# Scaling two query blocks from a two-byte copy, heads innermost, in a one-core kernel of linear attention and a state-space convolution

## The chip, the cores and the metric

The kernel runs on one core of a Trainium2 chip. A core has five engines that run side by side, each with its own instruction list in program order: TensorE (PE, matmuls; its weight loads are shown apart as PEld), VectorE (DVE), ScalarE (ACT), GpSimd (POOL) and SyncE (SP, which here only issues DMAs). They meet through semaphores. SBUF is the on-chip memory, PSUM the small memory that matmuls write and DVE and ACT read. The metric is the device time of one execution in microseconds (us), the median over several.

## What is computed

Two independent parts share the core, and their outputs stand side by side in the last axis (448 and 448 columns, 2048 rows):

```python
# part A: linear attention with a softmax feature map, H = 16 heads of Dh = 28
q, k, v = split(x @ wqkv)                     # x: 2048 x 448
pq, pk  = q @ w_phi[h], k @ w_phi[h]
phi_q = concat(softmax(pq), softmax(-pq))     # 56 features a head
phi_k = concat(softmax(pk), softmax(-pk))
kv  = phi_k^T v ;  z = sum over rows of phi_k
num = phi_q kv  ;  den = phi_q z + 1e-6
a   = (num / den) @ wo
# part B: S4 state-space convolution, 448 channels, 256 complex states
K = Re sum_n C_n B_n dt exp(dt A_n l)         # l = 0 .. 2047
b = causal convolution of u with K  +  u * Dskip
return concat(a, b)
```

## The kernel before

**Program and order.** The Python code first describes the work as about 1,565 small units (`plan.add`), each with its engine, or engines to choose from, and what it reads and writes. They run in an order that is written out by hand at the top of the file: the string `ORDER` gives for each place the unit's number and the engine that takes it (P for PE, V for DVE, A for ACT, G for POOL, S for SP), and `PLACES` says which PSUM buffer each PSUM tile gets (`mm`, `kb` or `arg`, two buffers each). An engine works its own entries off strictly in that order; a unit that waits holds up everything behind it on its engine. Copies out of PSUM (the helper `copy`, line 372 of the profile) and the sign flip (line 712) may stand on ACT or DVE; DMAs inside the core may be issued from SP, POOL or, late, ACT.

**Part B** runs from the start to the end of the span. The tables of exponentials and rotations are made in eight chunks of channels. For each, ACT evaluates Exp (`dampings`) and Sin (`rotations`) from PSUM (line 362), DVE multiplies the two into the table W (`damp`: two products, of 3,360 and 7,616 elements a partition; then a sign flip of half a block, the unit `neg`), DVE multiplies further powers into U (`hi_tables`), and PE joins W and U (`build_k`, two runs of 112 matmuls). The result is scattered through many small DMAs (`scatter_k`) into the kernel matrix Kt. Its spectrum (`kernel_spectrum`) is multiplied with the signal's on DVE (`conv_group`, three groups) and goes back through PE (`inverse`), from where copies and DMAs bring it out. The tables of the last chunk (7) are what the last group of the convolution waits for.

**Part A** is spread between. The query weights and key weights are folded with `w_phi` (`fold_weights`, which needs the tile `BD` that four small loads fill), keys are worked off in eight pairs (`key_pair`), and `key_end` masks the accumulated `kv` into the tile `KVN`. Then four query blocks of 512 rows follow (`query(sc)`, sc = 0 to 3), each in four tiles of 128 rows. A tile's steps are: eight matmuls write the numerators of both softmax halves into the PSUM tile `pn` (tag `arg`, f32, 128 x 2 x 448); DVE multiplies them with the scales `SC` (line 878, f32, one scale per row, half and head) and writes `on` in bf16; PE transposes `on` and adds the halves (`po`); a copy brings that to `oT_`; PE multiplies with the output weight `wo` (`pf`); a copy and a DMA from SP bring the tile out. Within `on` a head's 28 columns stand together: column = 28 * head + d. The rows of `wo` are loaded in the same order, by one DMA (`late1`).

The keys' scaling in `key_pair` already works in the other order: the four heads of a group of 112 columns stand innermost (column = 112 * c + 4 * d + h), and the factor is broadcast over d with the four heads contiguous. All its operands are bf16; it reads PSUM.

Of the kernel before, what the change touches and what calls it, by code (L numbers as in the profile page):

```python
# [63 lines left out]
def _dft_tables():  # L64
# [27 lines left out]
    for hh in range(4):  # L92
# [3 lines left out]
ORDER = ("23G 26P 39P 0A 48A 29P 24P 3S 1S 2S 4S 17G 8G 34P 27P 44P 43P 13S 192S 47P 49V 52V 51V 53V 50V 54P 55V 56P 57A "  # L96
# [200 lines left out]
def kernel(  # L297
# [537 lines left out]
    def query(sc, rank, phase, erank):  # L835
# [26 lines left out]
        for t4 in range(4):  # L862
# [10 lines left out]
            def num(t):  # L873
                return t[:, :, 0:D_MODEL].rearrange("p s (h d) -> p s h d", d=D_HEAD)

            def scaled(e, pn=pn, heads=heads, SC=SC, t4=t4):
# [4 lines left out]
                for s in range(2):  # L881
                    for h in range(N_HEAD):
                        nc.scalar.activation(heads[:, s, h], num(pn.t)[:, s, h], ACT.Copy, scale=SC[:, t4, s, h:h + 1])
# [276 lines left out]
```

## Time and profile before

| | us |
|---|---|
| median of 3 runs | 289.35 (289.08 to 289.59) |
| the profiled execution, whole | 289.75 |
| its span | 287.9 |
| DVE busy in the span | 268.4 |
| PE busy | 253.1 |
| ACT busy | 239.3 |
| 16 products of line 878 | 17.3 (mean 1.085 each) |

The span runs from the first to the last working instruction; the 1.85 us beside it belong to the execution's start and end. Busy times of one engine are the union of its instructions. Rows of a timeline give the start, the duration, the engine, the line, the operation with output and input, and the count; in brackets, the idle time of the engine before it and what ended it. Instructions on DVE and ACT overlap a little: the next starts before the one ahead has written its last element. The granted clock of PE was 0.992 of full speed over the span.

The 16 products of line 878 run in two bunches: the eight of blocks 0 and 1 from 158.9 to 194.9 us, the eight of blocks 2 and 3 from 211.4 to 247.7 us.

### The profile page before, as it was taken

Reading aid. Unit: us, or ns where it says so; the run is one execution under the profiler, and the core shown is the slowest. Engines: PE = TensorE matmul, PEld = TensorE weight load, DVE = VectorE, ACT = ScalarE, POOL = GpSimd, SP = SyncE. Lnnn points to the kernel's source line nnn. Section 1 sums busy time; section 2 is a strip of 40 time slices with the busy share of each in tenths; the row PEclk is TensorE's granted clock in tenths of the full one; section 3 lists DMA queues with packets and bytes.
Section 4 is the critical chain, followed back from the end, with each engine's and each line's share of the span. In section 5 each row is a group of like instructions: output and inputs, shape, how many; then the busy total and the mean of one; then the engine's idle time right before and its main releaser. Section 6 shows DMA issues by size and latency. Waiting matters only on the chain.

```text
span 287.9 us, 10151 instructions
## 1 busy us (share of the span) xinstructions
PE 253.1 (88%) x4280; PEld 202.6 (70%) x4280; DVE 268.4 (93%) x360; ACT 239.3 (83%) x537; POOL 82.8 (29%) x133
## 2 busy tenths in 40 slices
PE   7895798989978989979888889999899798999993
PEld 3454347668944778957755777769889687989983
DVE  2999997999999999999999999999999989799990
ACT  2999989999999999999999999999996162473241
POOL 2011024050604002030198232468250299000000
PEclk9999899999999999999999999999999999999999
DMA  6996333181546115142064255269969669786033
GB/s 186 298 268 179 71 96 82 24 207 27 84 81 138 32 29 107 34 100 61 11 116 70 56 113 141 54 112 293 238 137 287 224 163 242 222 270 227 18 128 130
DMA packets 41678, 38.54 MB, mean 134 GB/s; under 512 B 21168, under 2 KB 39000, under 8 KB 41506
## 3 DMA queue, kind: packets, MB, share of 16 engines
q1 hardware_dynamic: 33701, 30.14, 36.2%
q0 software_dynamic: 6480, 7.72, 14.9%
q8 instruction: 33, 0.54, 0.8%
q10 hardware_dynamic: 1453, 0.05, 0.3%
q14 instruction: 11, 0.09, 0.1%
HBM read 23.99 MB, written 7.34 MB: 109 GB/s over the span
## 4 chain that ended last, share of the span: by engine, by line
ACT 38%; DVE 23%; PE 14%; DMA 13%; issue 8%; SPq 2%; ACTq 1%; POOL 0%; DVEq 0%; POOLq 0%
ACT sbuf L362 29%; DVE sbuf L349 19%; PE mm L382 7%; ACT sbuf L372 6%; DMA sbuf<-sbuf 5%; PE kb L382 4%; DMA SUd<-sbuf 3%; SPq L397 2%; ACT L362 2%; DVE sbuf L372 2%; PE arg L382 2%; DMA sbuf<-in_B_u_dram 2%; DMA sbuf<-SUd 2%; DMA sbuf<-in_B_A_re_dram 1%; DVE sbuf L353 1%
## 5 line engine op out<-in xcount | busy, mean ns | idle before, releaser
L382 PEld LDWEIGHTS <-sbuf 128*32 128x32 bf16 (+4 forms) x4056 | 190.5, 119 | 72.5 <-issue 39.1
L349 DVE TENSOR_TENSOR sbuf<-sbuf 128x448 bf16<-128x448 bf16 (+9 forms) x213 | 205.3, 1007 | 2.6 <-ACT sbuf L372 1.8
L382 PE MATMUL mm<-sbuf 128*32 128x50 bf16 (+9 forms) x2676 | 157.0, 262 | 18.7 <-ACT sbuf L372 11.1
L362 ACT ACTIVATE sbuf<-arg 128x224 bf16<-128x224 f32 (+5 forms) x312 | 136.8, 676 | 0.1
L397 POOL DMA_DIRECT2D sbuf<-sbuf x99 | 65.0, 762 | 106.5 <-DVE sbuf L349 44.7
L372 ACT CAST sbuf<-mm 128x448 bf16<-128x448 f32 (+3 forms) x90 | 56.5, 657 | 21.5 <-PE mm L382 19.7
L382 PE MATMUL kb<-sbuf 128*32 128x50 bf16 (+10 forms) x790 | 64.6, 250 | 5.6 <-issue 2.0
L382 PE MATMUL arg<-sbuf 128*128 128x112 bf16 (+4 forms) x590 | 44.6, 225 | 1.4 <-ACT sbuf L362 1.2
L372 ACT CAST sbuf<-kb 128x448 bf16<-128x448 f32 (+4 forms) x42 | 24.2, 611 | 12.7 <-PE kb L382 11.0
L397 POOL DMA_DIRECT2D SUd<-sbuf x18 | 14.3, 827 | 45.4 <-ACT sbuf L372 35.9
L362 ACT ACTIVATE sbuf<-mm 112x512 bf16<-112x512 f32 x38 | 24.9, 798 | 0.0
L878 DVE TENSOR_TENSOR sbuf<-arg,sbuf 128x896 bf16<-128x896 f32 x16 | 17.3, 1085 | 1.3 <-PE kb L382 0.6
L362 ACT ACTIVATE sbuf<-sbuf 128x896 f32<-128x896 f32 (+3 forms) x13 | 13.0, 1038 | 1.8 <-DMA sbuf<-in_B_log_dt_dram 1.8
L362 ACT ACT_TABLE_LOAD x10 | 12.8, 1283 | 1.4 <-PEq L1144 1.2
L372 DVE CAST sbuf<-mm 128x448 bf16<-128x448 f32 (+2 forms) x17 | 10.1, 592 | 0.4 <-PE mm L382 0.3
L349 DVE TENSOR_TENSOR sbuf<-mm,sbuf 128x896 bf16<-128x896 bf16 (+1 forms) x17 | 9.3, 554 | 0.0
L812 PE MATMUL mm<-sbuf 112*128 112x112 bf16 x112 | 7.8, 212 | 1.7 <-DVE sbuf L807 0.9
L812 PEld LDWEIGHTS <-sbuf 112*128 112x128 bf16 x128 | 7.3, 97 | 2.7 <-issue 2.4
L372 DVE COPY sbuf<-kb 112x512 bf16<-112x512 bf16 (+1 forms) x18 | 7.2, 406 | 1.5 <-PE kb L584 1.5
L584 PEld LDWEIGHTS <-sbuf 128*112 128x112 bf16 x64 | 5.3, 129 | 3.9 <-issue 3.0
L584 PE MATMUL kb<-sbuf 128*112 128x128 bf16 x64 | 6.1, 219 | 2.2 <-DVE sbuf L372 1.3
L372 ACT CAST sbuf<-arg 128x224 bf16<-128x224 f32 (+1 forms) x10 | 3.5, 373 | 5.0 <-PE arg L382 5.0
(39 smaller groups left out, 69.9 us busy)
## 6 DMA issues: line engine op xcount, KB each, us to landing
sbuf<-const SPq DMA_DIRECT2D x37, 224.0 KB
sbuf<-sbuf POOLq DMA_DIRECT2D x21, 224.0 KB, 4.1
sbuf<-const SPq DMA_DIRECT2D x6, 512.0 KB
sbuf<-in_B_u_dram SPq DMA_DIRECT2D x6, 448.0 KB
sbuf<-in_A_x_dram SPq DMA_DIRECT2D x4, 448.0 KB
out_dram<-sbuf SPq DMA_DIRECT2D x16, 112.0 KB
sbuf<-SUd SPq DMA_DIRECT2D x1, 1792.0 KB
sbuf<-SUd SPq DMA_DIRECT2D x2, 896.0 KB
```

The source lines that it names most:

```text
L349: lambda: nc.vector.tensor_tensor(out=at(out_), in0=at(a), in1=at(b), op=op), [whose(a), whose(b)], [out_])
L353: lambda: nc.vector.scalar_tensor_tensor(out=at(out_), in0=at(a), scalar=sc, in1=at(b), op0=op0, op1=op1),
L362: lambda: nc.scalar.activation(at(out_), at(a), func, scale=scale, bias=bias),
L372: lambda e: (nc.scalar.copy if e == "ACT" else nc.vector.tensor_copy)(at(out_), at(a)), [whose(a)], [out_])
L382: nc.tensor.matmul(out_, lhsT=lhsT, rhs=rhs, start=start, stop=stop, **kw)
L397: plan.add({e: own[e] for e in engs}, lambda e=engs[0]: QUEUES[e].dma_start(out=out_, in_=in_, **kw), r, w, lat=lat, load=pieces / 16000 * ...
L584: mms(p, [lambda t, j=j, x=x: nc.tensor.transpose(t[:, j, :], x[:, 112 * j:112 * j + 112], ident[:, :]) for j in range(4)], 0.4, [x, ident ...
L812: mms(pt, [lambda t, i=i, s=s, c=c: nc.tensor.transpose(t[:, s, 112 * c:112 * c + 112], EKT[:, s, c, 128 * i:128 * i + 128], id112) for s ...
L878: nc.vector.tensor_tensor(out=heads, in0=num(pn.t), op=ALU.mult, in1=SC[:, t4].unsqueeze(3).to_broadcast([128, 2, 16, D_HEAD]))
```

## The change

1. In blocks 2 and 3 (`sc > 1`) ACT first copies the numerators of a tile from PSUM into a new bf16 tile `qc` (two buffers), and DVE then multiplies `qc` with the scales, which are bf16 in these blocks. In blocks 0 and 1 DVE still multiplies straight from PSUM in f32.
2. In all four blocks the four heads of a group stand innermost in `on`. For that `KVN` is written with heads innermost, and the rows of `wo` are loaded in the matching order, by four DMAs of 28 rows a group in place of one.
3. `ORDER` and `PLACES` are new throughout: 11 entries more (eight copies on ACT, three DMAs on SP), other places for many of the rest, and other engines for some copies, sign flips and DMAs. A branch of the code that no entry used is gone.

```diff
-    KVN = sb("KVN", [112, 2, 4, 4, D_HEAD], BF16, o1)
+    KVN = sb("KVN", [112, 2, 4, D_HEAD, 4], BF16, o1)
...
-    dma(["SP"], wo[:, :, :], A_wo.rearrange("(c p) n -> p c n", p=112), w=[wo[:, :, :]])
+    for h in range(4):
+        dma(["SP"], wo[h:112:4, :, :], A_wo.rearrange("(c h d) n -> h d c n", h=4, d=D_HEAD)[h], w=[wo[:, :, :]])
...
-            tt(KVN[:, s], (acc[s], lambda t: a4(t)[:, :, :, 0:D_HEAD]),
-               HM[:, :, 0:D_HEAD].unsqueeze(1).to_broadcast([112, 4, 4, D_HEAD]), ALU.mult)
+            tt(KVN[:, s], (acc[s], lambda t: t[0:112, 0:464].rearrange("p (c d h) -> p c d h", c=4, h=4)[:, :, 0:D_HEAD]),
+               HM[:, :, 0:D_HEAD].rearrange("p h d -> p d h").unsqueeze(1).to_broadcast([112, 4, D_HEAD, 4]), ALU.mult)
...
-        SC = sb("SC", [128, 4, 2, 16], F32, oSC, bufs=2)
+        SC = sb("SC", [128, 4, 2, 16], BF16 if sc > 1 else F32, oSC, bufs=2)
...
-            heads = on.rearrange("p s (h d) -> p s h d", d=D_HEAD)
...
-                    nc.vector.tensor_tensor(out=heads, in0=num(pn.t), op=ALU.mult,
-                                            in1=SC[:, t4].unsqueeze(3).to_broadcast([128, 2, 16, D_HEAD]))
...
+            def heads(t):
+                return t.rearrange("p s (c d h) -> p (s c) d h", c=4, h=4)
+            by = SC[:, t4].rearrange("p s (c h) -> p (s c) h", c=4).unsqueeze(2).to_broadcast([128, 8, D_HEAD, 4])
+            if sc > 1:
+                qc = sb("qc", [128, 2, D_MODEL], BF16, oV, bufs=2)
+                plan.add({"ACT": 0.8}, lambda pn=pn, qc=qc: nc.scalar.copy(qc[:, :, :], pn.t[:, :, 0:D_MODEL]), [pn], [qc[:, :, :]])
+                tt(heads(on), heads(qc), by, ALU.mult)
+            else:
+                tt(on, (pn, lambda t: t[:, :, 0:D_MODEL]), by, ALU.mult)
```

How the two lists assign what may stand on more than one engine (number of entries):

| units | before | after |
|---|---|---|
| sign flips (`neg`) on ACT / DVE | 4 / 4 | 1 / 7 |
| weight copies of `fold_weights` on ACT / DVE | 6 / 10 | 10 / 6 |
| table copies of `build_k` on ACT / DVE | 11 / 5 | 14 / 2 |
| x transposes' copies on ACT / DVE | 2 / 14 | 4 / 12 |
| copies of a query tile (`oT_`, `of`) on ACT / DVE | 29 / 3 | 31 / 1 |
| scatter DMAs of the last group issued by SP / POOL / ACT | 8 / 29 / 11 | 11 / 28 / 9 |
| loads of `BD` issued by SP / POOL | 4 / 0 | 0 / 4 |

More of the change, by code (lines that the diff above doesn't have):

```diff
@@ L94, in _dft_tables @@
     return tuple(_round_bf16(t) for t in (G, GI, FT, pid, hm))
-ORDER = ("23G 26P 39P 0A 48A 29P 24P 3S 1S 2S 4S 17G 8G 34P 27P 44P 43P 13S 192S 47P 49V 52V 51V 53V 50V 54P 55V 56P 57A "
[75 rows of a table removed]
-PLACES = ("kmmkmmmmkmkmmkmkkmmkmkkmmkmkmkmmmammkkmkkmkmkmkmkkkkmkmmkmkkmmmmkkkmmkmmkaakkmmakakmmkmakkmkmkmkmmkmmkmmmmamaamm"
-         "ammmammmmmmmmmmmmmmmamammammmmmmmmamamaamammmmammmmammmmmmammammmmmmmmmmkamkakaamkkammkakakkmkmmakmakammkkmkmamk"
-         "kammkmkmkkmammkmkkaammakmkmkmkkmamkmkamkmaammkmmkkmmamkmakmmkmmkkmmaammmakmkmkmmma")
+ORDER = ("23G 35P 37P 0A 48A 24P 43P 41P 31P 3S 1S 2S 13S 25P 44P 46P 8G 196G 17G 195S 6S 14S 49V 52V 53V 51V 50V 54P 55V "
[76 rows of a table added]
+PLACES = ("mkmmkmmkkkmkmkmmkkmmkmkmkmmmkkmmmmmkmmkkmkmkkmmkakkmkmkkmkkmmkmmkkmmmkmkmakmmakmamkmkakmmkmmkmmmkkmmmmmammmamama"
+         "mmmammmmmmmmmmmmmmmmmammammmammmmmmmmammamammmmmammmmammmmamammmmmaammkmkmaamkaakmkamkmaakkmkmkmakkamammkkmamkak"
+         "mkkmkkmkmkmmmmakkmamamkamkmkakkmmkamkamkkammkkmkmaakkmkmkkkkakkmkmaakkamkkmamkmmak")
 ENGINES = {"P": "PE", "V": "DVE", "A": "ACT", "G": "POOL", "S": "SP"}
@@ L870, in query @@
             on = sb("on", [128, 2, D_MODEL], BF16, oON, bufs=2)
-            heads = on.rearrange("p s (h d) -> p s h d", d=D_HEAD)
-            def num(t):
-                return t[:, :, 0:D_MODEL].rearrange("p s (h d) -> p s h d", d=D_HEAD)
-            def scaled(e, pn=pn, heads=heads, SC=SC, t4=t4):
-                if e == "DVE":
-                    nc.vector.tensor_tensor(out=heads, in0=num(pn.t), op=ALU.mult,
-                                            in1=SC[:, t4].unsqueeze(3).to_broadcast([128, 2, 16, D_HEAD]))
-                    return
-                for s in range(2):
-                    for h in range(N_HEAD):
-                        nc.scalar.activation(heads[:, s, h], num(pn.t)[:, s, h], ACT.Copy, scale=SC[:, t4, s, h:h + 1])
-            plan.add({"DVE": 0.065 + 2 * D_MODEL * 1.04e-3}, lambda scaled=scaled: scaled("DVE"), [pn, SC[:, t4]], [on[:, :, :]])
+            def heads(t):
[7 more added lines that the diff above has]
+                tt(on, (pn, lambda t: t[:, :, 0:D_MODEL]), by, ALU.mult)
             po = ps(("mm", "kb"), [112, 4, 128])
```

151 rows, old and new, of the table ORDER are left out of this document.

## The prediction

> **What bounds the kernel now.** I read the page's busy times first, then the busy time of each engine in stretches of 20 us, then the timelines of VectorE (DVE), ScalarE (ACT) and TensorE (PE) around the place where the bound changes hands.
>
> ```profile
> PE 253.1 (88%) x4280; PEld 202.6 (70%) x4280; DVE 268.4 (93%) x360; ACT 239.3 (83%) x537; POOL 82.8 (29%) x133
> ```
> ```profile
> 180.00:200.00 20.00, 19.43 (x275) 14.56 (x265) 20.00 (x25) 19.97 (x48) 13.90 (x23) 1.00 0.58 134
> 200.00:220.00 20.00, 19.00 (x399) 17.33 (x397) 19.57 (x31) 19.77 (x47) 6.32 (x10) 1.00 0.86 224
> 220.00:240.00 20.00, 17.41 (x391) 15.17 (x389) 19.20 (x13) 7.21 (x15) 11.11 (x21) 1.00 0.71 210
> 240.00:260.00 20.00, 18.41 (x266) 17.17 (x266) 18.25 (x14) 10.28 (x24) 4.95 (x9) 1.00 0.85 255
> 260.00:280.00 20.00, 19.41 (x324) 19.08 (x321) 19.73 (x21) 7.36 (x18) 0.00 (x0) 1.00 0.32 107
> ```
> The columns after the length are PE, weight loads, DVE, ACT and POOL. Up to about 213 us ACT has no gap and DVE hardly any; from 220 on ACT is half idle, while DVE and PE are both above 90%. So the time has two parts: up to the last Sin evaluation ACT's list decides, and after it PE's and DVE's lists, which are nearly equally full.
>
> **Prices.** Durations on a row overlap; what an instruction costs its engine is the distance to the next start ("step" below).
> ```profile
> 201.05 0.62 DVE L712 TENSOR_SCALAR sbuf<-sbuf 128x1680 bf16<-128x1680 bf16 x1
> 201.58 0.61 DVE L349 TENSOR_TENSOR sbuf<-sbuf 128x896 bf16<-128x896 bf16 x1
> 202.11 0.54 DVE L860 RECIPROCAL sbuf<-sbuf 128x64 f32<-128x64 f32 x1
> ...
> 215.30 4.11 DVE L349 TENSOR_TENSOR sbuf<-sbuf 128x7616 bf16<-128x7616 bf16 x1
> 219.34 2.08 DVE L878 TENSOR_TENSOR sbuf<-arg,sbuf 128x896 bf16<-128x896 f32 x2
> ```
> ```profile
> 54.89 1.13 ACT L362 ACTIVATE sbuf<-arg 128x896 bf16<-128x896 f32 x1
> 55.70 0.75 ACT L372 CAST sbuf<-mm 128x448 bf16<-128x448 f32 x1
> 56.12 1.32 ACT L362 ACTIVATE sbuf<-mm 112x512 bf16<-112x512 f32 x2
> ```
> ```profile
> 217.09 1.61 ACT L712 ACTIVATE sbuf<-sbuf 128x1680 bf16<-128x1680 bf16 x1
> 218.60 0.52 ACT L372 CAST sbuf<-kb 128x448 bf16<-128x448 f32 x1
> ```
> The f32 product of L878 steps 1.00 us (2.08 - 1.08), a product of 896 two-byte elements 0.53 (201.58 to 202.11). ACT reads 896 elements from PSUM in 0.81 (54.89 to 55.70) and 448 in 0.42. The sign flip of L712 costs ACT 1.51 (217.09 to 218.60) but DVE 0.53 (201.05 to 201.58).
>
> **The change, part by part.** *Numerators of query blocks 2 and 3.* Eight f32 products leave DVE (-8.0), eight two-byte ones come (8 x 0.53 = +4.25): -3.75 on DVE. Eight copies of 896 come to ACT: 8 x 0.81 = +6.5. All eight old products start after 211 us, where ACT is idle more than half the time, so the copies have cover; without it they cost what they add. The new product has no row of its own. The nearest is the key scaling, same broadcast of four heads innermost over 896 two-byte elements, 612 ns, as long as other two-byte products; the far end is the f32 row, 1.08 us, which would return all 3.75. I take 0.53.
>
> *Blocks 0 and 1* keep an f32 product with another traversal: 1.00 each, as now. The two KVN products (112x448) keep their count; a strided write is bounded by 0 and, at worst, another such duration each (609 ns, in all 1.2 us), once, near 155 us where ACT decides; I take 0.
>
> *Output weight.* One load becomes four on SP's queue, three more issues at some 0.45 us each (as SP's issues follow one another on its timeline); the first now stands behind other early loads, the others among the scatter issues. The tile is first read by block 0's last matmuls, long after; cover is the SP queue's slack. If it fails, the scatter behind is late by 1.3 us. I take 0.
>
> *Order lists.* Here lies more than in the edit. I counted both lists, each entry at its step. In whole: DVE -4.2, PE 0, ACT +3.3 (sign flips 4 to 1: -4.5; numerators +6.5; other copies +2.8; two DMA issues fewer -1.5). Table loads stay ten. The four loads for BD go from SP to POOL's queue, behind the gather, and the folding matmuls need them: four issues at 0.76 (the mean of L397 on POOL) could set these back 3.0, or free SP and gain as much; I take 0, as the folded weights are first used by the key exponentials near 45 us.
>
> Ahead of the last Sin evaluation on ACT: sign flips 3 to 0, -4.5; transposed-weight copies 6 to 10, +1.7; table copies 8 to 12, +1.6; x copies 2 to 4, +1.0; others -0.9. **Sum -1.2.** There the chunk's second damping product on DVE (7616 wide, 215.30) may start. DVE's list ahead of that product shrinks by 3.4 (two L878 products -2.0, table copies -1.3, fold copies -1.4, block copies -1.1, against sign flips +1.6 and small ones +0.8), so ACT, not DVE, will release it.
>
> *PE from there.*
> ```profile
> 220.34 2.74 PE L382 MATMUL mm<-sbuf 128*32 128x50 bf16 x112
> ...
> 226.32 2.35 PE L382 MATMUL kb<-sbuf 128*32 128x50 bf16 x60 [1.95 <-issue]
> ...
> 231.49 0.74 PE L382 MATMUL mm<-sbuf 128*128 128x224 bf16 x6 [0.54 <-ACT sbuf L372]
> ...
> 241.03 1.89 PE L382 MATMUL kb<-sbuf 128*128 128x224 bf16 x18 [1.13 <-ACT sbuf L372]
> ...
> 258.11 1.94 PE L382 MATMUL mm<-sbuf 128*128 128x112 bf16 x36 [0.55 <-DVE sbuf L349]
> ...
> 275.86 5.81 PE L382 MATMUL mm<-sbuf 128*128 128x112 bf16 x108 [0.44 <-DVE sbuf L349]
> ...
> 281.50 1.93 PE L382 MATMUL arg<-sbuf 128*128 128x112 bf16 x36
> ```
> From the last table build (220.34) to its end (283.43) PE spends 63.1 us: 58.5 of work, 1.95 waiting for nothing visible, and 0.54 + 1.13 on ACT and 0.55 + 0.44 on DVE. The new list puts two blocks behind that build that stood ahead of it (transposes of 2.0, 0.45, output product of 2.1, 0.76): +1.2 here, and -1.2 ahead. ACT's route to the build (last Sin, then numerator and spectrum copies, then the sign flip) allows a start 1 to 2 us earlier; PE's own list allows 1.2. I take -1.2 for the start.
>
> DVE reaches its last product about 4.4 us sooner if its waits stay: 2.8 at the damping product (212.5 instead of 215.3), 0.8 less work behind it, and two inverse copies of 0.8 moved past the end. So the DVE waits of PE go (-1.0), the ACT waits stay. Behind the last products PE has three inverse blocks instead of two, 1.8 more, which only a late DVE would expose. One output DMA instead of two follows the last copy: -0.4, an issue's length.
>
> **Sum:** start -1.2, PE list +1.2, waits -1.0, last DMA -0.4: **-1.4**. The profiled execution took 289.75 (span 287.9), 0.40 over the median of 289.35; so 288.35 for it and **287.95** as median. A measurement of this kernel can tell some 0.2%, 0.6 us, from nothing. Own range of this case: 286.7 to 288.7 (all visible PE waits gone, or only half of the DVE ones and no gain at the last DMA).
>
> **Rivals.** *DVE was the bound.* The chain of waits from 233 us on is mostly DVE, which speaks for it; PE's 19.41 busy of 20 us from 260 to 280 against. Then the last product comes 4.4 sooner, less 1.8 of PE's third block: -2.6, with the last DMA -3.0; where PE has hidden slack the 1.8 goes too. It gives 286.35, at best 284.6.
>
> *PE alone decides.* The same work, and the waits only move: -1.2 + 1.2 and nothing else, 289.35. For it: PE's list is not a matmul shorter.
>
> *ACT pays more than DVE saves (slower).* ACT serves its list in order. Now a numerator copy stands before each of the last table build's two copies, and others before the spectrum copies that free PSUM for PE and before ACT's scatter issues. If three of these hold PE by 0.81 each, that is +2.4 on the front gain -1.2 and list +1.2, with no other gain: 291.75. It decides as soon as these copies wait for their own matmuls instead of using idle ACT time. Against: 22.5 us of idle ACT time from 220 to 260 (40 less 7.21 and 10.28). [...]
>
> *The product is not fast from this layout:* +3.75 on DVE, half hidden by PE, 289.85. The key scaling speaks against.
>
> **Chances.** Forecast 0.40, DVE bound 0.21, PE alone 0.13, ACT pays 0.23, slow product 0.03. Faster by over 0.6 us: the first two, 0.61. Within 0.6: PE alone and half of the slow product, 0.14. Slower: 0.25. Range 285.4 to 291.2: it takes in most of the DVE case, the KVN and load bounds, and two of the three holds of the ACT case.
>
> **What would show it.** Right: 128x896 two-byte products near 612 ns on DVE with about 264 us busy; ACT near 243 with no gap before its last Sin; the last build on PE near 219; PE's DVE waits after 250 gone. Wrong: gaps on ACT before 210 us (the new order starves it, and every step shifts), PE idle on ACT copies after 230 growing past 3 us (ACT pays), or the last build starting no earlier.

## The result and the profile after

The changed kernel takes 307.65 us (median; 306.44 to 311.3), the kernel before 289.47 in the same comparison: ratio 1.0614 [1.0578, 1.065], 6% slower where 0.5% faster was forecast, and far outside the range. Now and then an execution of any of these kernels runs slower than the rest (here the one of 311.3): the ratios leave such executions out, the medians count all, and where the two differ a little, the ratio is used.

From the page of the changed kernel, its busy times and four rows of its 40 slices (one digit is a slice's busy share in tenths, for PEclk the granted clock):

```profile
PE 257.6 (84%) x4280; PEld 206.0 (67%) x4280; DVE 266.0 (87%) x355; ACT 245.0 (80%) x550; POOL 85.7 (28%) x138
...
PE   7686689796499988989519499899999989899994
...
DVE  3699999989679999997169689999999999999980
ACT  3699999989399999999618969999999958454321
...
PEclk9799999979599999999857969999999999999999
```

DVE is 2.4 us less busy than before and ACT 5.7 more: the edit itself did about what it says. But the span grew by 17.7 us (305.6 against 287.9) with nearly the same work in it. The new thing is in the slices: around the 11th and in the 20th and 21st all three engines are idle *together*, and PE's granted clock dips there too. Before, ACT had no gap from 40 to 213 us.

Busy times in stretches of 40 us (columns as in the prediction's table: length, PE, weight loads, DVE, ACT, POOL, granted clock, DMA share, GB/s), first two of the kernel before, then the changed kernel's:

```profile
60.00:100.00 40.00, 35.34 (x560) 27.83 (x559) 39.74 (x56) 39.94 (x102) 9.68 (x14) 1.00 0.43 92
...
140.00:180.00 40.00, 34.43 (x694) 26.80 (x695) 39.26 (x64) 39.96 (x93) 20.57 (x30) 1.00 0.44 91
```

```profile
60.00:100.00 40.00, 31.95 (x509) 24.74 (x510) 33.61 (x54) 34.15 (x91) 10.39 (x13) 0.87 0.40 83
100.00:140.00 40.00, 37.04 (x754) 30.81 (x753) 39.11 (x52) 39.94 (x101) 7.99 (x10) 1.00 0.26 55
140.00:180.00 40.00, 25.98 (x395) 17.58 (x394) 25.75 (x45) 26.69 (x63) 10.85 (x19) 0.76 0.25 50
180.00:220.00 40.00, 38.31 (x781) 31.18 (x780) 38.91 (x50) 39.43 (x94) 19.15 (x30) 0.98 0.55 128
220.00:260.00 40.00, 38.16 (x804) 33.94 (x803) 39.29 (x45) 34.01 (x71) 19.45 (x33) 1.00 0.82 238
260.00:300.00 40.00, 39.16 (x636) 37.72 (x634) 36.83 (x34) 17.57 (x42) 4.31 (x8) 1.00 0.54 166
```

ACT, which sets the pace up to its last Sin, lacks 5.9 us of 40 in one stretch and 13.3 in another: 19.2 together, about the whole loss. Where the prediction expected the change to act, from 220 us on, PE is as full as it was.

The view of waits names what ended these gaps (waiting engine and line, the releaser, total, times, longest):

```profile
POOL sbuf L398 <- DMA sbuf<-in_A_wo_dram: 23.8, 2, 16.5
...
DVE sbuf L350 <- DMA sbuf<-in_A_wo_dram: 14.3, 3, 8.5
...
ACT sbuf L363 <- DMA sbuf<-in_A_wo_dram: 10.3, 3, 6.9
...
PE mm L383 <- DMA sbuf<-in_A_wo_dram: 6.3, 1, 6.3
PE mm L383 <- issue: 6.3, 1, 6.3
...
PE kb L383 <- DMA sbuf<-in_A_wo_dram: 3.6, 1, 3.6
```

Every engine waits for a load of the output weight, which the instructions that wait do not read: on DVE they are mostly products for the tables, on ACT mostly evaluations of Exp and Sin. PE's wait that is put down to "issue" lies at the first of the four loads too (74.18 to 80.45 us; the load is issued at 77.55). Smaller rows of the same view bring the waits for these loads to 13.1 us on ACT; of its 19.2, another 5.1 are waits for PE soon behind such a stop, and 0.9 lie ahead of the first. One of the places, on the timelines of SP's queue, ACT, DVE and PE:

```profile
148.69 0.89 SPq L398 DMA_DIRECT2D sbuf<-in_A_wo_dram  x1
```
```profile
147.58 1.08 ACT L363 ACTIVATE sbuf<-arg 112x512 bf16<-112x512 f32 x2
151.46 0.45 ACT L373 CAST sbuf<-mm 128x350 bf16<-128x350 f32 x1 [2.79 <-DMA sbuf<-in_A_wo_dram]
```
```profile
142.38 0.63 DVE L350 TENSOR_TENSOR sbuf<-sbuf 128x896 bf16<-128x896 bf16 x1
151.47 2.91 DVE L350 TENSOR_TENSOR sbuf<-sbuf 128x3360 bf16<-128x3360 bf16 x2 [8.46 <-DMA sbuf<-in_A_wo_dram]
```
```profile
146.83 0.96 PE L383 MATMUL arg<-sbuf 128*128 128x112 bf16 x16
151.42 0.55 PE L383 MATMUL kb<-sbuf 128*112 128x116 bf16 x4 [3.63 <-DMA sbuf<-in_A_wo_dram]
```

Read the times across the four. DVE stops at 143.01, PE at 147.79, ACT at 148.66; at 148.69, with the last of them done, the load is issued; at 151.42 to 151.47 all three go on. So the load waited for all engines and then all engines waited for the load. It is a full stop of PE, ACT and DVE: each loses the time from its own last instruction ahead of the load to that of the slowest, and 2.8 us for the load.

What the built program's instructions wait for says the same. The issue of one of the four loads, in the changed kernel:

```
DMACopy sbuf<-in_A_wo_dram 28x4x448 [waits DMASW1,DMAHW0,DMASW0,DMAHW1,DVE,DMAHW3,PE,DMAHW4,Activation,Pool]
```

It waits for four engines and six DMA counters; the other three loads wait for PE, ACT and DVE and for some DMA counters. The load goes to `wo[h:112:4, :, :]`, every fourth partition of a region of the one large SBUF tile that holds nearly everything in this kernel. The idea to test: such a target is tracked as if it touched the whole tile.

### The profile page after: what moved, and what is told of

Its sections match the earlier page's. It is cut to its first block, busy times and chain, and to the rows that moved or that the text cites. A ratio compares the mean times of both kernels' runs of the same rounds, so it can differ in the third digit from the quotient of the medians.

```text
span 305.6 us, 10168 instructions
## 1 busy us (share of the span) xinstructions
PE 257.6 (84%) x4280; PEld 206.0 (67%) x4280; DVE 266.0 (87%) x355; ACT 245.0 (80%) x550; POOL 85.7 (28%) x138
## 5 line engine op out<-in xcount | busy, mean ns | idle before, releaser
L350 DVE TENSOR_TENSOR sbuf<-sbuf 128x896 bf16<-128x896 bf16 (+9 forms) x221 | 210.0, 993 | 15.7 <-DMA sbuf<-in_A_wo_dram 14.3
L383 PE MATMUL mm<-sbuf 128*32 128x50 bf16 (+10 forms) x2289 | 146.4, 265 | 28.4 <-ACT sbuf L373 6.8
L383 PE MATMUL kb<-sbuf 128*32 128x50 bf16 (+10 forms) x1147 | 76.6, 250 | 8.4 <-DMA sbuf<-in_A_wo_dram 3.6
L373 ACT CAST sbuf<-mm 128x448 bf16<-128x448 f32 (+3 forms) x78 | 51.7, 683 | 14.1 <-PE mm L383 10.7
L383 PE MATMUL arg<-sbuf 128*128 128x112 bf16 (+3 forms) x620 | 46.9, 228 | 0.9 <-ACT sbuf L363 0.9
L373 ACT CAST sbuf<-kb 128x448 bf16<-128x448 f32 (+4 forms) x51 | 28.8, 600 | 11.4 <-PE kb L383 6.3
L373 DVE CAST sbuf<-mm 128x448 bf16<-128x448 f32 (+1 forms) x16 | 9.6, 603 | 2.0 <-PE mm L383 2.0
L350 DVE TENSOR_TENSOR sbuf<-arg,sbuf 128x896 bf16<-128x896 f32 (+1 forms) x11 | 10.4, 955 | 0.9 <-PE arg L383 0.9
L879 ACT CAST sbuf<-arg 128x896 bf16<-128x896 f32 x8 | 8.0, 1020 | 1.6 <-PE mm L383 1.6
L373 DVE COPY sbuf<-kb 112x512 bf16<-112x512 bf16 (+2 forms) x16 | 7.1, 450 | 1.9 <-PE kb L594 1.3
```

What stands on the lines that cost most here:

```text
L350: lambda: nc.vector.tensor_tensor(out=at(out_), in0=at(a), in1=at(b), op=op), [whose(a), whose(b)], [out_])
L373: lambda e: (nc.scalar.copy if e == "ACT" else nc.vector.tensor_copy)(at(out_), at(a)), [whose(a)], [out_])
L383: nc.tensor.matmul(out_, lhsT=lhsT, rhs=rhs, start=start, stop=stop, **kw)
L879: plan.add({"ACT": 0.8}, lambda pn=pn, qc=qc: nc.scalar.copy(qc[:, :, :], pn.t[:, :, 0:D_MODEL]), [pn], [qc[:, :, :]])
```

## The experiments

Two theories were set against each other: that the stops come from how the strided loads are tracked (then the edit and its lists as such gain about what was forecast), and that the new order, the copies or the slow transfers cost the time.

**e1: the same rows of `wo`, written to neighbouring partitions.** The permutation is put on the DRAM side: one load for each group of 112 rows instead of one for each head of the groups.

```diff
-    for h in range(4):
-        dma(["SP"], wo[h:112:4, :, :], A_wo.rearrange("(c h d) n -> h d c n", h=4, d=D_HEAD)[h], w=[wo[:, :, :]])
+    for c in range(4):
+        src = bass.AP(tensor=A_wo.tensor, offset=A_wo.offset + 112 * c * D_MODEL,
+                      ap=[[D_MODEL, D_HEAD], [D_HEAD * D_MODEL, 4], [1, D_MODEL]])
+        dma(["SP"], wo[:, c, :], src, w=[wo[:, :, :]])
```

> The changed kernel, but the four loads of the output weight are cut by column group c and write 112 neighbouring partitions each, instead of every fourth partition; same bytes, same four places on SP, same order lists, same result. Theory (a load that writes every fourth partition of the one big SBUF tile is tracked as touching the whole tile, so it waits for every engine and every engine waits for it): all waits named in_A_wo_dram vanish; ACT's idle time between 20 and 220 us falls from 19.9 us to under 2; 286.5 to 289.5 us. Rival A (the transfers themselves land late): the gaps stay, over 300. Rival B (the new order lists starve the engines): ACT still shows gaps of 5 us and more before 210, over 295. Rival C (the numerator copies cost ACT more than DVE saves): gaps before 180 vanish but the time behind the last Sin grows; 291 to 294.

Measured: ratio to before 0.9943 [0.99, 0.9986], median 288.87 against 289.4. No engine waits for `in_A_wo_dram` any more, and the built program's issue waits for one DMA counter. Stretches of e1:

```profile
60.00:100.00 40.00, 36.85 (x608) 28.39 (x611) 39.53 (x56) 39.90 (x100) 12.49 (x17) 1.00 0.41 86
...
140.00:180.00 40.00, 35.83 (x700) 27.19 (x701) 38.87 (x60) 39.96 (x101) 15.80 (x25) 0.96 0.48 98
```

ACT is full again in both. The difference between the ratios, 1.0614 - 0.9943 = 0.067, is 19.4 us of 289.4 (by the two intervals some 1.6 either way): that is what the four loads cost. Lists, buffers, copies and products are the same in both kernels. With e5, which can't be told apart from it, e1 is the fastest version of this study.

**e5: the strided loads unchanged, `wo` in an SBUF tile of its own.**

```diff
-    wo = sb("wo", [112, 4, D_MODEL], BF16, ...)
+    wo = sb_pool.tile([112, 4, D_MODEL], BF16, name="wo")
```

The large tile is 3,584 bytes a partition shorter for it.

> The changed kernel with its four loads into every fourth partition as they are, but the output weight lies in an SBUF tile of its own, and the one big tile is 3,584 bytes a partition shorter. Theory (it is not the strided transfer that costs, but that the tracking takes it as touching the whole tile it writes to, which in the changed kernel is all of SBUF): no engine waits for in_A_wo_dram, 286.5 to 290 us, the same as e1 within 0.5%. Rival A (strided transfers land late or block the queue): 295 or more.

Measured: 0.9952 [0.9905, 0.9999], as e1. The four transfers are those of the changed kernel, no engine waits for them, and the built program's issue of the first waits for one DMA counter, as in e1. So neither the transfers nor the partitions that they write cost anything that can be measured here; the waits do that a strided target gets inside the shared tile. How the tracking comes to them isn't shown; their result is.

**e2: e1 and one strided load on top**, of 28 rows, ahead of the load for c = 0; the four regular loads write the same rows again.

```diff
+    nc.sync.dma_start(out=wo[0:112:4, :, :], in_=A_wo.rearrange("(c h d) n -> h d c n", h=4, d=D_HEAD)[0])
```

> As e1, plus one load of 28 rows into every fourth partition, in front of the first of the four (its rows are overwritten by the regular loads). Theory: one stop of all engines at that place, as the first stop of the changed kernel (ACT idle 2.9 + 2.1 us around 80 us): 4 to 6 us over e1. Rival A: 98 KB more through SP's queue alone, under 1 us over e1. Rivals B and C: no difference to e1.

Measured: 1.0208 [1.0137, 1.0279]; over e1 0.0265 x 289.4 = 7.7 us, rather more than expected. One stop is in its view of waits, at the place of the load:

```profile
POOL sbuf L398 <- DMA sbuf<-in_A_wo_dram: 15.3, 1, 15.3
DVE sbuf L350 <- DMA sbuf<-in_A_wo_dram: 3.0, 1, 3.0
ACT sbuf L363 <- DMA sbuf<-in_A_wo_dram: 2.8, 1, 2.8
```

The waits on DVE and ACT account for 3 of the 7.7 us. More comes behind it: PE stands still for 6.16 us here (72.92 to 79.08), so ACT finds no finished work of PE's to use, and 3 us later it waits 2.09 us for PE (2.07 in the changed kernel, at the same place). ACT's two waits make 4.9 us of the 5.7 by which the two profiled executions differ (spans of 290.8 and 285.1); what the averages have beyond that wasn't traced.

**e3: the kernel before, with one strided load of 28 natural rows** ahead of the regular load that overwrites it; and **e6, its control**, the same rows to `wo[0:28]`.

```diff
+    nc.sync.dma_start(out=wo[0:112:4, :, :], in_=A_wo.rearrange("(c d h) n -> h d c n", h=4, d=D_HEAD)[0])
```

> The kernel before, with its own order lists, plus one load of 28 rows of the output weight into every fourth partition right ahead of its regular load on SP (which then writes the same rows again). Theory: one stop of all engines near 88 us, 3 to 8 us slower than before, with waits named in_A_wo_dram on DVE, ACT and PE. Rivals A, B and C: within 1 us of before.

> Control for e3: the kernel before plus a load of the same 28 rows, same bytes, same place on SP, but into 28 neighbouring partitions. Theory: within 1 us of before, no wait named in_A_wo_dram on DVE, ACT or PE. Rival A: as slow as e3, some 7 us over before.

Measured: e3 1.024 [1.0167, 1.0313], +6.9 us; e6 1.0059 [1.002, 1.0099], +1.7 us, somewhat more than expected, with no engine waiting for the load. On the timeline of DVE in e3 the stop is plain (ACT waits 1.1 us here, PE 2.15):

```profile
87.75 0.18 DVE L736 TENSOR_SCALAR sbuf<-sbuf 128x112 bf16<-128x112 bf16 x1
96.30 1.91 DVE L349 TENSOR_TENSOR sbuf<-sbuf 128x3360 bf16<-128x3360 bf16 x1 [8.36 <-DMA sbuf<-in_A_wo_dram]
```

So the stop needs nothing of the change: one line in the old kernel, with the old lists, makes it. Why e6 costs 1.7 us stays open: its profiled execution is as fast as that of before.

**e9: the four strided loads issued one right behind the other**, at the first one's place (the first unit issues all four, the other three nothing). One stop or four?

> The changed kernel with its four loads into every fourth partition issued one right behind another, at the place of the first of them, instead of at four places; nothing else differs. Theory (each place where such a load stands among other work costs one stop: until the slowest engine has caught up, the load has landed and the engines have filled again): one stop remains, a little longer as four loads land, so 6 to 9 us over e1, 293.5 to 297. Rival A (each strided transfer costs): as the changed kernel, 305 or more.

Measured: 1.0267 [1.0175, 1.0358], over e1 0.0324 x 289.4 = 9.4 us: a little over what was expected. The trace has one stop, of 5.7 us on DVE, 5.6 on ACT and 9.0 on PE, not four. Here the cost goes by how often the engines are stopped at different places (19.4 us for four places, 9.4 for the same four loads at one) more than by the number of transfers (7.7 for one load in e2).

**e4: the edit in the old lists.** Before's `ORDER` and `PLACES`, with `wo` loaded as in e1; the rest of the edit is as in the change, and each copy is issued right ahead of its product.

```diff
-                    nc.vector.tensor_tensor(out=heads, in0=num(pn.t), op=ALU.mult,
-                                            in1=SC[:, t4].unsqueeze(3).to_broadcast([128, 2, 16, D_HEAD]))
...
+                    nc.scalar.copy(qc[:, :, :], pn.t[:, :, 0:D_MODEL])
+                    nc.vector.tensor_tensor(out=heads(on), in0=heads(qc), in1=by, op=ALU.mult)
```

> The kernel before with its old order lists and engine choices, and the whole edit in it: numerators of blocks 2 and 3 copied by ACT right ahead of their product, two-byte product, heads innermost, the output weight's rows reordered (loaded by four contiguous loads at the old place). It parts the edit from the order lists. Theory (the edit is worth up to the DVE waits of the end, at no more than a copy's delay each): 287.5 to 290, DVE busy 3.7 us less, ACT busy 6 to 8 us more. Rival C: 290.5 or more.

Measured: 1.0043 [1.0007, 1.0079], median 291.06: 0.4% slower than before, and 1% slower than e1. DVE is 3.3 us less busy, 265.1, but now waits for the copies, 6.8 us in four waits. DVE's and ACT's timeline at the first of them:

```profile
208.75 0.61 DVE L372 CAST sbuf<-kb 128x448 bf16<-128x448 f32 x1
213.07 0.63 DVE L884 TENSOR_TENSOR sbuf<-sbuf 128x896 bf16<-128x896 bf16 x1 [3.72 <-ACT sbuf L883]
```
```profile
210.27 1.98 ACT L362 ACTIVATE sbuf<-arg 128x112 bf16<-128x112 f32 x5
211.84 1.20 ACT L883 CAST sbuf<-arg 128x896 bf16<-128x896 f32 x1
```

ACT's list is full until its last Sin, and the copy comes when the list comes to it; DVE idles 3.72 us ahead of a product that saves it 0.47 (a step of 0.53 instead of 1.00). So in the old lists the gain is gone, as the prediction's rival "ACT pays" has it, though in another way: DVE waits for the copies, and PE, which the rival had held for 2.4 us, only for 0.74. Only one product follows each copy. Whether a copy pays for itself in the new lists, where ACT has room (busy 23.32 of the 40 us from 220 to 260 in e1), e7 leaves open. That the copies alone make the kernel slower isn't shown. The profiled execution of e4, its fastest, is no longer than that of before, and e4 issues three loads more at the place where one more cost 1.7 us in e6.

**e7: e1 without the copies.** The f32 product straight from PSUM in all blocks, at the same places of the lists, with heads innermost.

```diff
-        SC = sb("SC", [128, 4, 2, 16], BF16 if sc > 1 else F32, oSC, bufs=2)
+        SC = sb("SC", [128, 4, 2, 16], F32, oSC, bufs=2)
...
-                plan.add({"ACT": 0.8}, lambda pn=pn, qc=qc: nc.scalar.copy(qc[:, :, :], pn.t[:, :, 0:D_MODEL]), [pn], [qc[:, :, :]])
-                tt(heads(on), heads(qc), by, ALU.mult)
+                plan.add({"ACT": 0.8}, lambda: None, [pn], [qc[:, :, :]])
+                tt(on, (pn, lambda t: t[:, :, 0:D_MODEL]), by, ALU.mult)
```

> e1 without the numerators' copies: ACT's eight copies are left out, and DVE multiplies from PSUM in f32 in all blocks, at the same places of the new lists. It gives what the copies bring inside the new lists. Theory (behind the last Sin DVE and PE decide and ACT has room): DVE busy 3.7 us more, ACT 6.5 to 8 less, 1 to 3 us slower than e1. Rival C (ACT pays more than DVE saves): the same as e1 or faster.

Measured: 1.046 [1.0386, 1.0533], some 15 us over e1 where 1 to 3 were expected. The expectation was wrong, and the timeline of PE says why:

```profile
220.09 0.91 PE L383 MATMUL arg<-sbuf 112*128 112x112 bf16 x8 [3.62 <-DVE sbuf L350]
...
243.99 0.91 PE L383 MATMUL arg<-sbuf 112*128 112x112 bf16 x8 [3.62 <-DVE sbuf L350]
```

In the new lists the copy empties the PSUM tile early, and the product can stand much later on DVE, behind a damping product. Without the copy the buffer stays taken until that product, and PE waits for it, 10.1 us in three waits. So this kernel doesn't measure the copy's own worth inside the new lists, and that stays open; it shows what else the copy does there.

**e8: e1 with heads outermost.** The bf16 copy and product stay; the scale is then the same for 28 neighbouring elements (broadcast innermost). `KVN` and the rows of `wo` are as before.

```diff
-            def heads(t):
-                return t.rearrange("p s (c d h) -> p (s c) d h", c=4, h=4)
-            by = SC[:, t4].rearrange("p s (c h) -> p (s c) h", c=4).unsqueeze(2).to_broadcast([128, 8, D_HEAD, 4])
+            def heads(t):
+                return t.rearrange("p s (h d) -> p s h d", d=D_HEAD)
+            by = SC[:, t4].unsqueeze(3).to_broadcast([128, 2, 16, D_HEAD])
```

> e1 with heads outermost, as in the kernel before (masked key sums, output weight's rows and the product's traversal), while ACT still copies the numerators of blocks 2 and 3 to two bytes and all operands of the product have two bytes. The scale then stands still over 28 elements. Theory of the prediction (the heads must stand innermost for the fast product): the eight products take 1.08 us instead of 0.61, 1 to 3 us slower than e1. Rival (two-byte operands are enough): 0.61 us and the time of e1.

Measured: 1.0068 [1.0023, 1.0113], 3.6 us over e1, somewhat more than expected. The two-byte products of 896 elements, grouped by form (total busy, mean ns; then idle before), of e8 and of e1:

```profile
L350 DVE TENSOR_TENSOR sbuf<-sbuf 128x896 bf16<-128x896 bf16 x82 | 52.5, 664 | 0.3
```
```profile
L350 DVE TENSOR_TENSOR sbuf<-sbuf 128x896 bf16<-128x896 bf16 x82 | 48.6, 615 | 1.5 <-PE mm L383 1.1
```

Eight of the 82 are the ones that differ: 52.5 - 48.6 = 3.9 us more, 0.49 each, so some 1.10 us a product, the price of the f32 one (1.08). Here two bytes alone gain DVE nothing; with heads innermost as well the same product takes 0.61, so the layout is what makes it fast.

## Why the prediction was wrong

**The step that failed is *Output weight*.** The prediction put it so: "cover is the SP queue's slack. If it fails, the scatter behind is late by 1.3 us. I take 0." The four loads cost 19.4 us (changed kernel against e1). What was counted was the length of three more issues and what stands behind them on SP; what an issue *waits for*, and who then waits for it, was taken to be as for the one load before. Its target had changed from 112 neighbouring partitions to every fourth, and that was enough (e3: one line, +6.9 us; e5: the same loads, no stop). The bound of 1.3 us was a bound on the wrong quantity (and the issues themselves take 0.86 to 0.99 us, not 0.45). The profile of before couldn't show it, as nothing there stops all engines in this way; the list of what the built program's instructions wait for could.

With that step mended (e1), the forecast of 287.95 stands against 0.9943 x 289.35 = 287.7. Step by step, on e1's trace (one execution, 287.03 us, where the median is 288.87):

- *Numerators, blocks 2 and 3*: right. Eight more two-byte products at 615 ns (0.53 a step was taken from the key scaling's 612). DVE's busy time falls by 3.0 us to 265.3; "about 264" was forecast.
- *ACT*: 244.2 us busy; near 243 was forecast. It has 0.6 us of gaps from 20 to 220 us. The gaps that the prediction named as a sign of trouble did show in the changed kernel, but they came from the loads and not, as it supposed, from the new order.
- *KVN*: 902 ns a product (915 in the changed kernel) instead of 609, 0.6 us in all, inside the bounds of 0 and 1.2, but there is no strided write, which the prediction named: what has steps now is the mask, read with heads innermost, 58 bytes apart.
- *Start of the last table build*: 219.03 instead of 220.34, -1.3 where -1.2 was taken. The damping product ahead of it starts at 213.62; 212.5 was forecast. The last Sin on ACT, which releases it, ends only 0.3 us sooner than before (213.58 against 213.85), where 1.2 was taken; PE's shorter list ahead of the build is there.
- *PE from there*: the fall of the waits was undersized. On PE's timeline of e1 the last build, all rows with an idle time in brackets, and the last row:

```profile
219.03 2.94 PE L383 MATMUL mm<-sbuf 128*32 128x50 bf16 x112
...
224.84 1.20 PE L383 MATMUL kb<-sbuf 128*32 128x50 bf16 x44 [1.31 <-issue]
...
229.65 0.74 PE L383 MATMUL kb<-sbuf 128*128 128x224 bf16 x6 [0.48 <-ACT sbuf L373]
...
235.46 1.16 PE L383 MATMUL mm<-sbuf 128*128 128x112 bf16 x20 [0.18 <-DMA sbuf<-const]
...
271.70 1.93 PE L383 MATMUL kb<-sbuf 128*128 128x112 bf16 x36 [0.30 <-DVE sbuf L350]
...
279.05 1.89 PE L383 MATMUL kb<-sbuf 128*128 128x224 bf16 x18
```

From 219.03 to 280.94 are 61.9 us, 2.3 of them waits, so 59.6 of work: the +1.2 of the list is there (58.5 before, 59.7 forecast). The waits fell from 4.6 to 2.3, not by the 1.0 taken: DVE's part by 0.7, ACT's, which the prediction had left as it was, by 1.2, and the rest by 0.5. That makes the sum for this one execution -1.3 + 1.2 - 2.3 and some at the end, 2.7 us below before's profiled one; over many executions it is 0.0057 x 289.4 = 1.65 us, and 1.4 was forecast. That these two lie so close is in part luck: by its interval e1 gains anything from 0.4 to 2.9 us, far wider than the 0.6 us that the prediction thought a measurement could tell, and in the one trace the terms add up to about twice the forecast.

Some figures of the prediction are off without changing it: the parts of the sum ahead of the last Sin make -1.1, not -1.2; from 220 to 240 us PE is busy 17.41 of 20, under 90%; ACT does have gaps in the first 40 us; and by the terms it names, its own range would run from 286.3 to 288.85.

Of the rivals, *ACT pays* is seen in part in the old lists (e4: the gain is gone) and not in the new, *the slow product* holds with heads outermost (e8) and not here. None of them contained the stops.

## What to carry to other kernels

- Ahead of a change to where a DMA writes, look at what the built program makes it wait for and what then waits for it, not only at the place of its issue. A target of strided partitions in a tile that others share can stop every engine, here at 5 to 8 us a stop (19.4 for four, 7.7 and 6.9 for one); put the permutation on the DRAM side (e1, 0.9943 of before), or give the target a tile of its own (e5, 0.9952).
- Ahead of moving work to another engine, see whether that engine's list has room at that place: in the old lists DVE waited 6.8 us for ACT's copies (e4). The lists can matter as much as the edit: nearly the same edit gave 0.4% slower in the old lists and 0.6% faster in the new, and what the new lists gain without it wasn't measured. Ask also what the moved step frees early; lists made around that no longer work without it.

## What the runs showed of the hardware

- PE's granted clock falls with the stops: 0.87 and 0.76 in the two stretches of 40 us with stops, 0.98 to 1.00 in the others from 100 us on. In steps of 4 us it is 0.50 from 76 to 80 us, in which PE does nothing, 0.85 from 148 to 152, 0.50 from 152 to 164, and 0.50 again from 176 to 180, soon after the last load; PE's three longest waits for these loads, of 6.28, 3.63 and 6.33 us, end at 80.45, 151.42 and 159.47. But it is 0.76 and 0.82 from 60 to 68 too, ahead of the first load, so the stops aren't all of it. The kernel before has 1.00 in all such steps from 60 to 88 and from 140 to 168. PE's busy time is 2.6 us longer than in e1 for the same 4,280 matmuls, but e8, without a stop, has the same busy time (257.8 us, mean clock 0.967), so what the clock adds to the 19.4 us isn't shown.
- The KVN product reads its mask at steps of 58 bytes now (before, its PSUM operand was the one with steps), and a product of 448 elements takes 1.5 times as long (915 ns against 609). In e8, with heads outermost again, it takes 624 ns. Before and in the changed kernel:

```profile
L349 DVE TENSOR_TENSOR sbuf<-kb,sbuf 112x448 bf16<-112x448 f32 x2 | 1.2, 609 | 0.0
```
```profile
L350 DVE TENSOR_TENSOR sbuf<-kb,sbuf 112x448 bf16<-112x448 f32 x2 | 1.8, 915 | 0.0
```

  The order of the PSUM operand changed together with the mask's, and no other step was run, so the share of each isn't shown.
